# Holding the loads of a second weight matrix behind a store of finer x sums

## The chip, the cores and the metric

The kernel runs on one core of one Trainium2 chip. The metric is the device time in microseconds (us). The engines are named as the profile names them: PE is the matrix engine and PEld its weight loads, DVE the vector engine, ACT the scalar engine, POOL the GpSimd engine and SP the engine that does nothing here but issue DMAs. DMAs issued by SP travel on queue q1 of the profile, those issued by POOL on queue q0.

## The reference

A linear attention is followed by a mixture of eight experts, whose routing table is normalized by eight rounds of alternating row and column sums:

```python
# attention, per batch and head: q, k, v are (8, 8, 576, 64), w_phi is (64, 128)
proj = x @ w_phi
proj = proj - max(abs(proj), axis=-1)
phi = concatenate([exp(proj), exp(-proj)])
kv = k_p.T @ v;  z = k_p.sum(over tokens)
attn = (q_p @ kv) / (q_p @ z + 1e-06)
# experts: x is attn as (N, D) = (4608, 512), E = 8, F = 1024
logits = x @ w_gate
P = exp(logits - logits.max())
for _ in range(8):
    P /= P.sum(1, keepdims=True) + 1e-09
    P /= P.sum(0, keepdims=True) + 1e-09
    P *= N / E
out = 0
for e in range(E):
    h = maximum(x @ w1[e], 0)        # w1[e] is (512, 1024)
    out += P[:, e:e+1] * (h @ w2[e]) # w2[e] is (1024, 512)
```

## The kernel before

The program is first written down as a list of operations, each with the engine that does it, an estimated duration, and the keys that it reads and writes. `Plan.schedule` then simulates all engines and the DMA queues with these estimates, and always takes next the operation that can start first by its own clock, ties going to the one that was written down first. The order that comes out is the order of each engine's instruction stream. On the chip every engine works through its stream in that order; where it needs another engine's result or a landed DMA, it waits on a semaphore, and everything behind it on the same engine waits too. Waits for tiles come from the tile framework; `Op.behind` adds one by hand.

The attention takes about the first 200 us. In it, and for some 45 us after it, PE also works on expert 0 with plain matmuls (L622). From then on experts 1 to 7 are computed with a scheme of seven block products in place of eight, in nine units per expert (two for each pair of token groups (0,1), (2,3), (4,5), (6,7), and one for group 8 alone). This needs sums and differences of blocks of x and of the weights, which DVE makes with `sub` (L1240):

- `sums_x` makes three sums for a pair (into three of the four buffers of the ring X), and stores them to DRAM tiles `xd` (`move_x`, L1422). For three of the blocks of x, named 11, 21 and t1, it calls `fine_x`, which stores the block itself (L1369, L1371) and makes four finer sums of it in one more buffer of ring X, which are stored from there to the DRAM tiles `xi` (L1385; the tile of block t1 appears as `xi0t`, `xi2t`, `xi4t` and `xi6t`, by the pair's first group). With three buffers held by the coarser sums, the finer sums of 11, 21 and t1 take turns in the one that is left: DVE may start on one when the store of the one before has landed.
- Experts 2 to 7 read these sums back from DRAM (`load_fine`, L1397). Expert 1 uses those just made.
- `sums_up` and `sums_down` make the sums of the weights of an expert. `sums_up` of expert 1 follows the finished routing table P; its `sums_down` is written down after the first pair's two units.

`routing` does the eight rounds for P on DVE: row sums (L1164), their reciprocals (L1166), the scaled table (L1167), column sums (L1170), a split into bf16 parts (L1179), a small PE matmul that adds over the partitions (`ps<-cs,colw`, 24 columns), and then L1185, L1188 and L1161. Between them stand DVE's work for expert 0 (L1025) and the x sums of pair (0, 1).

The weights of experts 1 to 7 are loaded by `load_w`, two DMAs of 1 MB (as bf16; from fp32 in DRAM) issued by POOL one straight after the other. `w1` and `w2` have two buffers each; one of each lies in a tile called `wx`, which the attention uses before. So expert 1's weights appear as `wx`, and expert 2's as `w`. POOL's other work in the experts is adding products to the output table (`acc<-acc,hx`, L1875) out of two buffers V that ACT fills (L1872), and smaller sums (L1643).

The main loop begins so:

```python
for e in range(1, E):
    w1, w2 = load_w(e, ["late", ("acc", 4, 0, 0)] if e > 1 else ["late"])
    if e == 1:
        nextX = sums_x(pairs[0])
    A7 = sums_up(e, w1)
    B7 = sums_down(e, w2) if e > 1 else None
```

Of the kernel before, what the change touches and what calls it, by code (L numbers as in the profile page):

```python
# [349 lines left out]
def kernel(  # L350
# [11 lines left out]
    nc = tc.nc  # L362
# [32 lines left out]
    acc = [accp.tile([128, 4, DD], FP32, name=f"acc{g}", tag=f"acc{g}") for g in range(NA)]  # L395
# [12 lines left out]
    late = {}  # L408
# [19 lines left out]
    def dma(queue, nbytes, rate, fn, r=(), w=()):  # L428

        speed, unit = LINK.get(rate, (rate, 40))  # L430
        if nbytes == 2 << 20:
            speed, unit = 400, 150
        o = plan.op(queue, 0.8 if queue == "POOL" else 0.6, 0.0, fn, r, w, (), nbytes / speed)
        o.turn, o.unit = rate == 148, unit

    TI, GR, KM, QM, PM, NM, RM = 0, 0, 0, 0, 0, 0, 0
    R = {}
# [68 lines left out]
    def new(tag):  # L506
        return R[tag].new()
# [3 lines left out]
        return buf().bitcast(BF16)  # L511


    def load_w(e, r=()):
        w1, w2 = new("w1"), new("w2")
        for w, src in ((w1, moe_w1), (w2, moe_w2)):
            dma("POOL", 2 << 20, 280, lambda w=w, src=src: nc.gpsimd.dma_start(
                out=w(), in_=src[e].rearrange("(c p) f -> p c f", p=128)),
                r, [(w, i, j) for i in range(2) for j in range(2)])
        return w1, w2  # L520

    def load_w0(i, r):
# [508 lines left out]
    for b in range(2):  # L1031
# [4 lines left out]
        w=["wphi_f0"])  # L1036
    dma("ACT", 1 << 15, 100, lambda: nc.scalar.dma_start(out=wphi_f[64:128, :], in_=w_phi),
        w=["wphi_f1"])
# [13 lines left out]
    for i in range(2):  # L1052
        dve(450, lambda i=i: nc.vector.memset(vrd[i], 0.0),
            w=[("vrd", i, h, *y) for h in range(2) for y in ((), (1,))])
# [79 lines left out]
    o = plan.op("X", 0.0, 0.0, swap, w=["late"])  # L1134
# [101 lines left out]
    def sub(eng, el, out_, x, y, op, r, w):  # L1236
        f = nc.vector if eng is dve else nc.gpsimd
        kw = {"shared": True} if eng is dve else {}
        eng(el * 0.5 if eng is dve else el * 1.04 + 128,
            lambda: f.tensor_tensor(out=out_(), in0=x(), in1=y(), op=op), r, w, **kw)  # L1240

    def sums_up(e, w1):

        def q(i, j):
            return lambda: w1()[:, 2 * j:2 * j + 2, 512 * i:512 * i + 512]

        S = [None] + [new("T") for _ in range(3)]

        def s(n):
            return lambda: S[n]().rearrange("p (a b) -> p a b", a=2)  # L1250


        a11, a12, a21, a22 = (1, 0), (1, 1), (0, 0), (0, 1)
        late = ["late"] + (["P"] if e == 1 else [])

        def k(a):
            return [(w1, *a)]

        sub(dve, 1024, s(2), q(*a11), q(*a21), ALU.subtract, k(a11) + k(a21) + late, [S[2]])
        sub(dve, 1024, q(*a21), q(*a21), q(*a22), ALU.add, k(a22) + late, k(a21))  # L1260
        sub(dve, 1024, s(1), q(*a21), q(*a11), ALU.subtract, k(a21) + k(a11) + late, [S[1]])
        sub(dve, 1024, s(3), q(*a12), s(1), ALU.subtract, k(a12) + [S[1]] + late, [S[3]])
        A = {"11": (q(*a11), k(a11)), "12": (q(*a12), k(a12)), "22": (q(*a22), k(a22)),
             "s1": (q(*a21), k(a21)), "s2": (s(1), [S[1]]), "s3": (s(2), [S[2]]),
             "s4": (s(3), [S[3]])}
        if e > 1:
            for n in INNER:
                fine_up(A, n)
        return A
# [48 lines left out]
    def xq(gs, i, j):  # L1318

        n = len(gs)  # L1320
        return lambda: xT[:, 2 * i:2 * i + 2, 512 * gs[0]:512 * (gs[0] + n)].rearrange(
            "p k (a b) -> p a k b", a=n)[:, :, :, 256 * j:256 * j + 256]

    def xall(gs):
        return [k for g in gs for k in xkeys(g)]
# [12 lines left out]
    class Turns:  # L1338
# [4 lines left out]
        def next(self):  # L1343
# [16 lines left out]
    Xi = {(g[0], n): dram.tile([128, 7, 256], BF16, name=f"xi{g[0]}{n}")  # L1360
          for g in pairs for n in INNER.values()}
# [3 lines left out]
    def fine_x(gs, n, b, r0):  # L1365

        g = gs[0]
        r = xall(gs) + ["late", *r0]
        dma("SP", 1 << 16, 160, lambda: nc.sync.dma_start(  # L1369
            out=Xi[g, n][:, 0, :], in_=b()[:, 0, 0, :]), r, [("Xi", g, n, 0)])  # L1370
        dma("SP", 1 << 17, 160, lambda: nc.sync.dma_start(  # L1371
            out=Xi[g, n][:, 1:3, :], in_=b()[:, :, 1, :]), r, [("Xi", g, n, 1)])
        y = new("X")

        def t(n):
            return lambda: y().rearrange("p a k c -> p (a k) c")[:, n]

        def blk(k, a):
            return lambda: b()[:, a, k, :]

        sub(dve, 256, t(0), blk(0, 1), blk(0, 0), ALU.subtract, r, [(y, 0), "order of X"])
        sub(dve, 256, t(2), blk(1, 1), blk(0, 1), ALU.subtract, r, [(y, 2)])
        sub(dve, 256, t(1), blk(1, 1), t(0), ALU.subtract, [*r, (y, 0)], [(y, 1)])
        sub(dve, 256, t(3), blk(1, 0), t(1), ALU.subtract, [*r, (y, 1)], [(y, 3)])
        dma("SP", 1 << 18, 160, lambda: nc.sync.dma_start(  # L1385
            out=Xi[g, n][:, 3:7, :], in_=y().rearrange("p a k c -> p (a k) c")),
            [(y, i) for i in range(4)], [("Xi", g, n, 2)])

# [27 lines left out]
    def new_x():  # L1416
        return {n: new("X") for n in (2, 3, 4)}
# [10 lines left out]
    def sums_x(gs, r0=()):  # L1428

        X = new_x()  # L1430

        def x(n):
            return lambda: X[n]()[:, 0:len(gs)]

        b11, b12, b21, b22 = (xq(gs, *ij) for ij in ((0, 1), (0, 0), (1, 1), (1, 0)))
        el, keys = 512 * len(gs), xall(gs)
        r = keys + ["late", *r0]
        sub(dve, el, x(3), b22, b12, ALU.subtract, r, [X[3], "order of X"])
        sub(dve, el, b12, b12, b11, ALU.subtract, ["late", *r0], keys)
        sub(dve, el, x(2), b22, b12, ALU.subtract, r, [X[2]])  # L1440
        sub(dve, el, x(4), b21, x(2), ALU.subtract, r + [X[2]], [X[4], "order of X"])
        for n in (3, 2, 4):
            move_x(gs, n, True, X)
        if len(gs) == 2:
            for n, b in (("22", b22), ("11", b11), ("21", b21), ("t1", b12)):
                if n in INNER.values():
                    fine_x(gs, n, b, r0)
                else:
                    for a in range(2):
                        dma("SP", 1 << 17, 160, lambda n=n, a=a, b=b: nc.sync.dma_start(  # L1450
                            out=Xp[gs[0], n][:, a], in_=b()[:, a]), r, [("Xp", gs[0], n, a)])
        return X
# [524 lines left out]

    early, dn = [plain(8)], plain(7)
    for e in range(1, E):
        w1, w2 = load_w(e, ["late", ("acc", 4, 0, 0)] if e > 1 else ["late"])  # L1980
        if e == 1:
            nextX = sums_x(pairs[0])
        A7 = sums_up(e, w1)
        B7 = sums_down(e, w2) if e > 1 else None
        turn = [*pairs, (8,)] if e < E - 1 else [(8,), *pairs]
        if e == 2:
            o = plan.op("X", 0.0, 0.0, lambda: None, w=["K"])
            for d in plan.ops[:-1]:
                if any(b.ring is R["X"] for b in d.bufs):
                    d.users.append(o)  # L1990
                    o.deps.append(d)
                    o.left += 1
        for n, gs in enumerate(turn):
            if (e, n) == (1, 4):
                plan.inorder = 1
            X = nextX if e == 1 else load_fine(gs)
            H = {g: [] for g in gs}
            for fp in range(len(gs)):
                hs = take()
                for i, z in enumerate(hs):  # L2000
                    H[gs[min(i, len(gs) - 1)]].append(z)
                fine = e > 1 and len(gs) == 2
                if fine:
                    un = up49(A7, fp, X, H, gs, ["up0", "K"])
                else:
                    un = up7(A7, gs, fp, X, H, ["up0"])
                for o in UNITS[turns.pop(0)]:
                    if o in un:
                        un[o]()
                    elif len(o) == 3:  # L2010
                        un[o[:2], int(o[2])]()
                    elif dn is not None:
                        dn[o]()
                if dn is not None:
                    dn["out"]()
                    slots.extend(dn["slots"])
                if e == 1 and fp == 0 and n + 1 < len(turn):
                    nextX = sums_x(turn[n + 1], [(H[gs[0]][0], 0, 1, 1)])
                if B7 is None and fp:
                    B7 = sums_down(e, w2)  # L2020
                if fp == len(gs) - 1:
                    wait += [(e, g, H[g], B7, w2, [z.ring.number for z in H[g]]) for g in gs]
                dn = next_down()
# [35 lines left out]
```

## Time and profile before

| | us |
|---|---|
| median of 3 runs | 1011.01 |
| lowest and highest run | 1009.40 and 1012.25 |
| the profiled execution, its own time | 1010.62 |
| span of the profiled execution | 1008.8 |
| PE busy | 994.0 (99% of the span), 8376 matmuls |
| DVE busy | 898.6 (89%) |
| ACT busy | 812.8 (81%) |
| POOL busy | 447.6 (44%) |
| q1 (issued by SP and ACT) | 103.33 MB, 36.3% of the 16 DMA engines' span |
| q0 (issued by POOL) | 23.86 MB, 16.9% |

All times inside a run are us from the start of the span. A busy share says how long an engine had an instruction in work; PE's matmuls overlap, so its busy time can hide gaps shorter than a matmul's duration, and the starts of the matmuls are the finer measure: a matmul of 512 columns starts 0.216 us after the one before where PE runs without a gap. The granted clock is 1.00 in the whole run. A timeline row gives start, duration, engine, line, operation, tiles, shapes and count, and in brackets the idle time before it and what ended that.

### The profile page before, as it was taken

How to read it: one execution, taken by the hardware profiler on the slowest of the kernel's cores; microseconds unless marked ns; L12 is line 12 of the kernel's file. 1: busy time of each engine (PE TensorE's matmuls, PEld its weight loads, DVE VectorE, ACT ScalarE, POOL GpSimd, SP SyncE). 2: the span in 40 equal slices, each digit the busy share in tenths (PEclk: the TensorE clock that was granted, in tenths of full speed). 3: DMA queues.
4: the chain of work that ended last, by engine and by line, in shares of the span. 5: the costliest groups of instructions: out<-in, count | busy, mean ns of one | idle time of the engine just before them, and what ended most of it. 6: DMA issues, size and time to landing. Idle time of an engine off the chain costs nothing.

```text
span 1008.8 us, 23309 instructions
## 1 busy us (share of the span) xinstructions
PE 994.0 (99%) x8376; PEld 727.7 (72%) x8376; DVE 898.6 (89%) x1999; ACT 812.8 (81%) x1930; POOL 447.6 (44%) x514
## 2 busy tenths in 40 slices
PE   7899999999999999999999999999999999999998
PEld 5666666644566877777777877787778777787775
DVE  7999998987888998899989898989889988989886
ACT  7999999845979788878878788777887888778874
POOL 5778674400133344434444444444443444344443
PEclk9999999999999999999999999999999999999999
DMA  9999999181136423282327133632246222724653
GB/s 249 183 202 183 157 153 144 38 170 56 53 121 143 147 97 98 84 184 96 109 98 170 44 100 131 130 127 98 97 117 177 97 98 84 147 79 142 208 174 126
DMA packets 129748, 128.86 MB, mean 128 GB/s; under 512 B 55776, under 2 KB 98272, under 8 KB 129632
## 3 DMA queue, kind: packets, MB, share of 16 engines
q1 hardware_dynamic: 97680, 103.33, 36.3%
q0 software_dynamic: 31648, 23.86, 16.9%
q8 instruction: 65, 1.06, 0.5%
q14 instruction: 51, 0.42, 0.2%
q10 hardware_dynamic: 304, 0.20, 0.1%
HBM read 122.50 MB, written 19.53 MB: 141 GB/s over the span
## 4 chain that ended last, share of the span: by engine, by line
PE 92%; DVE 3%; ACT 2%; DMA 2%; issue 1%; POOL 0%; DVEq 0%
PE ps L1466 41%; PE ps L1475 20%; PE ps L622 17%; PE ps L1607 11%; PE ps L905 2%; DMA xi6t<-X 1%; DMA xi<-X 1%; PE ps L752 1%; ACT q L618 0%; DVE m L614 0%; ACT k L618 0%; DVE wx L614 0%; DVE X L1240 0%; DMA acc<-in_k_dram 0%; DVE hs L1676 0%
## 5 line engine op out<-in xcount | busy, mean ns | idle before, releaser
L1875 POOL TENSOR_TENSOR acc<-acc,hx 128x512 f32<-128x512 f32 x186 | 236.1, 1276 | 404.7 <-ACT hx L1872 135.0
L1466 PEld LDWEIGHTS <-hs 128*128 128x128 bf16 x1984 | 194.1, 98 | 46.4 <-issue 0.2
L1872 ACT ACTIVATE hx<-ps,P 128x256 f32<-128x256 f32 x372 | 158.9, 483 | 53.4 <-PE ps L1466 52.0
L1860 DVE SCALAR_TENSOR_TENSOR acc<-ps,P,acc 128x256 f32<-128x256 f32 x372 | 162.2, 478 | 30.2 <-PE ps L1466 28.2
L1475 PE MATMUL ps<-xT,T 128*128 128x512 bf16 x608 | 171.0, 379 | 0.0
L1466 PEld LDWEIGHTS <-hx 128*128 128x128 bf16 x1488 | 145.6, 98 | 24.9
L1466 PE MATMUL ps<-hx,hs 128*128 128x256 bf16 x992 | 144.3, 273 | 0.0
L1676 DVE CUSTOM_DVE_ANT_0 hs<-ps,U 128x512 bf16<-128x512 f32 x192 | 124.7, 684 | 11.3 <-PE ps L1475 6.6
L1607 PE MATMUL ps<-xT 128*128 128x256 bf16 x576 | 125.4, 272 | 0.0
L1475 PEld LDWEIGHTS <-T 128*128 128x128 bf16 x672 | 65.8, 98 | 40.6
L1682 ACT ACTIVATE hs<-ps 128x512 bf16<-128x512 f32 x96 | 55.9, 598 | 41.7 <-PE ps L1475 40.2
L1466 PE MATMUL ps<-wx,hs 128*128 128x256 bf16 x560 | 78.4, 273 | 0.0
L622 PE MATMUL ps<-w,hx 128*128 128x512 bf16 x288 | 73.0, 379 | 0.0
L622 PE MATMUL ps<-xT,w 128*128 128x512 bf16 x288 | 72.9, 379 | 0.0
L1466 PE MATMUL ps<-wx,hx 128*128 128x256 bf16 x496 | 72.3, 273 | 0.0
L1676 DVE CUSTOM_DVE_ANT_0 hs<-ps,X 128x512 bf16<-128x512 f32 x96 | 65.1, 684 | 7.8 <-PE ps L1607 6.9
L1466 PE MATMUL ps<-hx 128*128 128x256 bf16 x496 | 71.2, 273 | 0.0
L1607 PEld LDWEIGHTS <-xT 128*128 128x128 bf16 x576 | 56.3, 98 | 17.5
L1466 PE MATMUL ps<-w,hx 128*128 128x256 bf16 x432 | 62.2, 273 | 0.0
L614 DVE TENSOR_REDUCE m<-ps 128x4 f32<-128x512 f32 x88 | 58.8, 680 | 3.7 <-PE ps L622 1.9
L1672 ACT COPY X<-ps 128x512 f32<-128x512 f32 x96 | 58.6, 610 | 2.5 <-DVE ps L1650 2.5
L1466 PE MATMUL ps<-w,hs 128*128 128x256 bf16 x432 | 60.2, 273 | 0.0
(174 smaller groups left out, 2256.0 us busy)
## 6 DMA issues: line engine op xcount, KB each, us to landing
xT<-xi SPq DMA_DIRECT2D x48, 448.0 KB, 4.6
xT<-xd SPq DMA_DIRECT2D x72, 256.0 KB, 4.0
wx<-in_moe_w_dram POOLq DMA_DIRECT2D x8, 1024.0 KB, 11.2
v_m<-in_v_dram SPq DMA_DIRECT2D x15, 512.0 KB, 5.2
out_dram<-acc SPq DMA_DIRECT2D x14, 512.0 KB, 3.0
w<-in_moe_w_dram POOLq DMA_DIRECT2D x6, 1024.0 KB, 11.0
xT<-xp SPq DMA_DIRECT2D x24, 256.0 KB, 2.8
qk<-in_k_dram POOLq DMA_DIRECT2D x12, 256.0 KB, 5.4
```

The source lines that it names most:

```text
L614: dve(el, lambda: nc.vector.tensor_reduce(out=dst(), in_=src(), axis=AX.X, op=ALU.max, apply_absolute_value=True), r, w)
L622: nc.tensor.matmul(out_, lhsT=lhsT, rhs=rhs, start=start, stop=stop)
L905: pe(65, lambda j=j: nc.tensor.matmul(pn()[:, j * D1:j * D1 + D1], lhsT=s["T"][x]()[:, j % 2, 2 * h + j // 2, :] if j < 4 else r["T"][x]() ...
L1466: pe(256, lambda i=i, k=k, z=z: nc.tensor.matmul(bank()[:, 256 * i:256 * i + 256], lhsT=lhs(k, i), rhs=rhs(k), start=first and z, stop=k = ...
L1475: pe(512, lambda k=k: nc.tensor.matmul(bank().rearrange("p (a b) -> p a b", a=2), lhsT=lhs(k), rhs=rhs(k), start=first and k == 0, stop=k ...
L1607: pe(256, lambda: nc.tensor.matmul(halves_of(bank[q], n)(), lhsT=lhs(), rhs=t()[:, rhs, :], start=start, stop=True, skip_group_check=True) ...
L1672: act(512, lambda: nc.scalar.copy(out=flat(to[q])(), in_=bank[q]()), [bank[q]], [(to[q], 0), (to[q], 1)])
L1676: dve(515, lambda: nc.vector._custom_dve(ADD_SAT, out=out_(q, i, j), in0=bank[q]().rearrange("p (a b) -> p a b", a=2), in1=to[q](), s0=3.0 ...
L1682: act(512, lambda: nc.scalar.activation(out=out_(q, i, j), in_=bank[q]().rearrange("p (a b) -> p a b", a=2), func=ACT.Relu, bias=0.0, scal ...
L1860: dve(320, lambda n=n, ts=ts: nc.vector.scalar_tensor_tensor(out=acc[g][:, ts, 256 * j:256 * j + 256], in0=bank()[:, 256 * n:256 * n + 256 ...
L1872: act(370, lambda n=n: nc.scalar.activation(out=u()[:, n, :], in_=bank()[:, 256 * n:256 * n + 256], func=ACT.Copy, bias=0.0, scale=P[:, 4 ...
L1875: pool(695, lambda: nc.gpsimd.tensor_tensor(out=acc[g][:, 2 * i:2 * i + 2, 256 * j:256 * j + 256], in0=acc[g][:, 2 * i:2 * i + 2, 256 * j: ...
```

## The change

`load_w` gets a third argument, the key of a store. The load of `w2` now reads that key for the planner (so it is planned behind the store's landing), and is given `behind`, a real wait on the chip for the landing of that store. The store is that of the four finer sums of block t1: for expert 1 that of pair (0, 1) (`xi0t<-X`), for expert 2 that of pair (6, 7) (`xi6t<-X`). Experts 3 to 7 have none. So that the store is known, `sums_x` of the first pair is now written down ahead of `load_w` for expert 1; and `dma` returns its operation.

```diff
@@ dma
         o.turn, o.unit = rate == 148, unit
+        return o
@@
-    def load_w(e, r=()):
+    written = {}
+
+    def load_w(e, r, store):
         w1, w2 = new("w1"), new("w2")
-        for w, src in ((w1, moe_w1), (w2, moe_w2)):
-            dma("POOL", 2 << 20, 280, lambda w=w, src=src: nc.gpsimd.dma_start(
+        for w, src, behind in ((w1, moe_w1, None), (w2, moe_w2, store)):
+            o = dma("POOL", 2 << 20, 280, lambda w=w, src=src: nc.gpsimd.dma_start(
                 out=w(), in_=src[e].rearrange("(c p) f -> p c f", p=128)),
-                r, [(w, i, j) for i in range(2) for j in range(2)])
+                r + ([behind] if behind else []),
+                [(w, i, j) for i in range(2) for j in range(2)])
+            o.behind = written.get(behind)
         return w1, w2
@@ fine_x
-        dma("SP", 1 << 18, 160, lambda: nc.sync.dma_start(
+        written["Xi", g, n, 2] = dma("SP", 1 << 18, 160, lambda: nc.sync.dma_start(
             out=Xi[g, n][:, 3:7, :], in_=y().rearrange("p a k c -> p (a k) c")),
             [(y, i) for i in range(4)], [("Xi", g, n, 2)])
@@ the main loop
     for e in range(1, E):
-        w1, w2 = load_w(e, ["late", ("acc", 4, 0, 0)] if e > 1 else ["late"])
         if e == 1:
             nextX = sums_x(pairs[0])
+        r = ["late", ("acc", 4, 0, 0)] if e > 1 else ["late"]
+        w1, w2 = load_w(e, r, ("Xi", 6 * (e - 1), "t1", 2) if e < 3 else None)
         A7 = sums_up(e, w1)
```

What this does to the engines' streams, beside the two waits, is small. On POOL the load of expert 2's `w2` stands one L1875 later than before. On DVE the finer sums of blocks 21 and t1 of pair (0, 1) stand earlier among the rounds of the routing: the first of 21 now directly ahead of the column sums (L1170) of the third round, where it stood behind the L1179 of the fourth. On PE the third and the fourth of the eight small matmuls `ps<-cs,colw` each stand two 512-column matmuls later, and two blocks of expert 0 change places. ACT and SP issue the same instructions in the same order. From there to the end every stream is the same, but for four PSUM banks that have changed names.

## The prediction

> **What bounds the kernel now.** I read the page's busy row first, then PE's waits after the attention, because a change that touches nothing before 203 us can only win what PE loses behind it.
>
> ```profile
> PE 994.0 (99%) x8376; PEld 727.7 (72%) x8376; DVE 898.6 (89%) x1999; ACT 812.8 (81%) x1930; POOL 447.6 (44%) x514
> ```
>
> ```profile
> PE ps L1475 <- DVE hs L1530: 0.6, 1, 0.6
> PE ps L622 <- DVE cs L1179: 0.4, 1, 0.4
> ```
>
> PE is busy 99% of the span, and behind 200 us the list of its waits has two entries. Busy time hides short gaps, so I also took the starts of all matmuls and subtracted the pace without gaps (0.216 us for 512 columns, 0.1085 for 256). At the first wait PE loses 0.52 us at 227.4 and 0.13 at 228.6; at the second 0.79 at 329.2 and 0.17 at 330.4. That is 1.6 us in all, and the rest of the 800 us behind them has hardly a gap. **No version of this change can win more than about 1.6 us, 0.16%.**
>
> Next, the timeline around both places, DVE, PE and the loads:
>
> ```profile
> 203.41 1.74 POOL L517 DMA_DIRECT2D wx<-in_moe_w_dram  x2 [7.21 <-PE ps L622]
> 217.08 0.32 SPq L1385 DMA_DIRECT2D xi<-X  x1
> 223.50 0.49 DVE L1240 TENSOR_TENSOR X<-xT 128x256 bf16<-128x256 bf16 x2 [1.49 <-DMA xi<-X]
> 228.10 0.19 PE L622 MATMUL ps<-cs,colw 128*128 128x24 bf16 x1 [0.36 <-DVE cs L1179]
> 316.00 1.69 POOL L517 DMA_DIRECT2D w<-in_moe_w_dram  x2
> 317.00 0.32 SPq L1385 DMA_DIRECT2D xi6t<-X  x1
> 324.77 0.42 DVE L1240 TENSOR_TENSOR X<-xT 128x512 bf16<-128x512 bf16 x1 [1.01 <-DMA xi6t<-X]
> 330.20 1.19 PE L1475 MATMUL ps<-X,wx 128*128 128x512 bf16 x4 [0.62 <-DVE hs L1530]
> ```
>
> Both waits of PE have one pattern. POOL issues two weight loads; a store of finer sums issued during them takes long to land (217.08 to 223.48, 6.40 us; 317.00 to 324.75, 7.75 us, where such stores take 2.0 us at other times); DVE stands idle for the buffer (1.49 and 1.01 us); and what DVE makes then comes late for PE.
>
> The third view is a window of 2 us (busy time of the five engine rows, granted clock, share of the DMA engines, GB/s), and the fourth the landings of the POOL loads of the tiles `wx` and `w`.
>
> ```profile
> 220.00:222.00 2.00, 2.00 (x11) 0.94 (x10) 1.83 (x6) 0.87 (x2) 0.00 (x0) 1.00 1.10 364
> ```
>
> ```profile
> DMA to landing us min/median/max: 10.4/13.8/17.2
> DMA to landing us min/median/max: 9.5/11.9/14.3
> ```
>
> By single DMAs, expert 1's are issued at 203.41 and 204.25 and land at 213.77 and 221.47; expert 2's at 316.00 and 316.79 and land at 325.55 and 331.10. So the two go one after the other: q0's bytes reach 1.05 MB at 212.6 and 2.10 MB at 220.3. While they last the stores get 0.07 to 0.1 MB/us; when the second is through, 0.31 to 0.37 (the 364 GB/s of the row 220 to 222).
>
> **Expert 1's hold.** What it removes: `w2` no longer moves from 212.6 to 220.3. What it doesn't: `w1` is in front, so up to 212.6 all is as before, and q1 has then moved 0.32 MB. Adding the stores in SP's order, the 256 KB store `xi<-X` of block 11 (217.08 before) ends at 1.77 MB. 1.77 less 0.32 at 0.34 MB/us takes 4.3 us: its bytes are through at 216.9. SP can issue it in time: it waits for the store eight places ahead (0.52 MB, through at 213.2, landed about 1.2 us later by the landings before), so at about 214.4. Landings follow the last byte by 0.8 to 1.2 us: it lands between 217.6 and 218.0, in place of 223.48.
>
> But the order now asks for it sooner. DVE's first finer sum of block 21 stands ahead of the third round's L1170, which before started at 216.69. So DVE waits there from 216.67 to about 217.8, in the middle of the rounds, where before it waited after the fourth round. From that landing to the third small matmul it is 0.2 us for the sub, 1.21 for L1170 to the second L1179 with two subs between (the same sequence took 207.92 to 209.13), and 0.09 of latencies: 1.50, so 219.3. PE, which ran it at 218.03, now stands two matmuls of 0.216 later: 218.46. PE loses 0.84 us. The fourth comes 20 matmuls (4.34 us) later for PE, at 223.6, and DVE has it ready at about 223.3 (c_bc to the next L1179 took 218.62 to 222.02, 3.4 us). The fifth: PE at 228.4, DVE at about 228. So the 0.65 lost at 227 to 229 goes, and 0.84 comes 9 us earlier: **+0.2 us**. The bounds: a landing before 216.96 costs nothing and gives -0.65; one 0.5 us later than 218.0 gives +0.9.
>
> The load itself: the t1 store lands about 226.6 (DVE is through with it some 4 us earlier than the 228.80 of its issue before, and it takes 2.0 us), POOL issues then in 0.87 us, and by the 9.5 to 10.4 us of a first load it lands about 237. DVE reads it first at 259.15, PE at 266.35: 22 us of cover, which is what would have to go before this costs anything. On POOL nothing else is queued until the L1875 at 269.95.
>
> **Expert 2's hold.** Here the first load, too, is in front of the store. By 324.5 q0 had moved 0.99 MB, all of it `w1`; so the store's 7.75 us were spent beside `w1` alone, and holding `w2` doesn't shorten them. DVE's 1.01 us and PE's 0.96 stay: **0**. The other bound is -0.96, if the mere queueing of `w2` held the store back.
>
> New is that POOL stands at the wait from 320.95 (the end of the L1875 that starts at 319.68) to 324.75, then issues for 0.87 us; the second L1875 of that pair, before at 320.95, starts at 325.63. Who waits for that: ACT's next fill of a V buffer, at 332.80, so 5.9 us of cover behind its end at 326.9. But it now falls into a run of DVE subs from 324.77 to 329.5 without a gap, which ends in the L1530 that PE waits for at 330.20. What POOL and DVE do to each other the trace shows nearby:
>
> ```profile
> 342.25 1.27 POOL L1875 TENSOR_TENSOR acc<-acc,hx 128x512 f32<-128x512 f32 x1 [1.17 <-ACT ps L1527]
> 342.62 1.18 DVE L1240 TENSOR_TENSOR hs<-hs 128x512 bf16<-128x512 bf16 x1
> 338.43 1.24 DVE L1240 TENSOR_TENSOR xT<-w,xT 128x256 bf16<-128x256 bf16 x1
> ```
>
> The sub at 342.62 takes 1.18 us, its kind 0.42 otherwise, and ends 0.28 after the POOL add; that at 338.43 takes 1.24 for 0.29. Between 275 and 343 I find six such subs, at 0.33 to 0.95 us too long, mean 0.63. DVE is the chain here, so PE pays it: **+0.6**, between 0 (the add slips into a gap) and 1.27 (a whole add). [...]
>
> `w2` of expert 2 lands at about 335 to 337 rather than 331.10; DVE reads it at 365.2. It now runs beside the loads `xT<-xi` issued from 329.99 and takes some us from them; these landed at 333.57 to 341.57, and PE's first uses are at 348.9, 349.1 and 351.2, 14 to 15 us behind the landings of their blocks. Nothing.
>
> **The sum.** +0.2 +0.6 = +0.8 on the profiled execution: 1010.62 to 1011.4. That execution lies 0.4 below the median, 1011.01, so for the median 1011.8. Both are inside 0.3% (3.0 us), about what a measurement of this kernel can tell from no change.
>
> **Rivals.** (1) The waits vanish. If the store lands before DVE asks, expert 1 gives -0.65; if expert 2's store is also quicker without the queued `w2` and the POOL add does no harm, another -0.96: 1010.4 to 1009.4. For it: the stores run at four times the pace as soon as `w2` is out of the way. Against it: the 216.9 above, and `w1` still being there both times. 30%. (2) Slower: the wait moved into the rounds is long. DVE now stops at 216.67 for a landing whose time before was 223.48, and from 216.96 on each us of its delay is one of PE's. Were the stores not sped up at all, PE would stand 6.5 us, less 0.65: 1016.9. It passes 0.3% if the landing is later than 220.6. For it: at 215 to 219 eight stores are queued, and SP's own waits for landings space them. Against it: at 220.3, with the loads through, 0.7 MB went in 2 us. 8%. (3) The hold is idle, both waits of PE stay as they are: 1011.0, 7%. My forecast has 55%.
>
> **How the numbers follow.** The low end is rival 1 in full, -1.6: 1009.4. The high end takes both upper bounds, +0.9 and +1.27, and a little of the 1.2 us by which the runs lie above the median: 1013.4. The chance of slower by over 0.3% is rival 2's, 8%; faster by over 0.3% exceeds what PE loses at these places and could only be scatter, 3%; the rest, 89%, is within.
>
> **What would show it.** Right: DVE's wait for `xi<-X` stands ahead of a column sum at 217 to 218, of 1 us, and PE waits 0.6 to 1.1 for the third `ps<-cs,colw`, none at 228; `xi6t<-X` takes over 7 us again; an L1875 starts at about 325.6 and a sub near it is 0.3 to 1 us too long. Wrong: `xi<-X` landing before 217 or after 220.6; `xi6t<-X` landing by 321; a wait of PE at a place that has none now, above all for `w` or `hx` behind 332, where POOL's delayed add would be the cause.

## The result and the profile after

| | before | after |
|---|---|---|
| median (18 runs each, us) | 1010.12 | 1012.41 |
| lowest and highest run | 1009.25, 1012.25 | 1011.23, 1015.05 |
| ratio of the times | | 1.0025, 95% interval 1.0017 to 1.0032 |
| profiled execution, its own time and span | 1010.62, 1008.8 | 1011.88, 1010.1 |

The change costs a quarter of a per cent: it is slower, and by the medians the loss lies inside the 0.3% that the forecast called "within". The line numbers of after are 5 higher (the POOL add L1875 is now L1880, a `sub` L1245, PE's second wait L1480 on L1535). The busy row of the page, in which 36 of PE's matmuls have no record, and PE's waits behind 200 us:

```profile
PE 991.9 (98%) x8340; PEld 727.8 (72%) x8376; DVE 900.1 (89%) x1999; ACT 813.4 (81%) x1930; POOL 448.2 (44%) x514
```

```profile
PE ps L1480 <- DVE hs L1535: 2.1, 1, 2.1
PE ps L627 <- DVE cs L1184: 0.3, 1, 0.3
PE ps L1471 <- DVE hx L1245: 0.3, 1, 0.3
```

The two waits of before, 0.6 and 0.4, have become one of 2.1 and two of 0.3 (of these the one on `cs` stands at expert 1's place, the one on `hx` at expert 2's). By the starts of the matmuls, with the pace taken off as in the prediction, PE loses 0.45 us at expert 1's place (0.65 before) and 0.43 + 2.29 + 0.17 = 2.89 at expert 2's (0.96 before). That is -0.20 and +1.93. The rest of the stream runs as before, except that this execution comes 0.41 us earlier out of the attention, which the change does not touch: -0.20 + 1.93 - 0.41 = 1.32, and the spans differ by 1.3.

Expert 1's place in the timeline (start, duration, engine, line, operation, tiles, and in brackets the idle time before it and what ended it):

```profile
217.00 0.29 DVE L1245 TENSOR_TENSOR X<-xT 128x256 bf16<-128x256 bf16 x1 [0.76 <-DMA xi<-X]
217.21 0.67 DVE L1175 TENSOR_REDUCE cs<-T 128x8 f32<-128x288 f32 x1
...
226.02 0.89 POOL L520 DMA_DIRECT2D wx<-in_moe_w_dram  x1 [22.18 <-DMA xi0t<-X]
```

The store that DVE waits for was issued at 213.79 and landed at 216.98, 6.5 us sooner than before. DVE now waits ahead of the column sum L1175 of the third round, 0.76 us, as the new order asks for. The held load goes out at 226.02, lands at 236.06, and nobody waits for it.

Expert 2's place, POOL, DVE and PE:

```profile
324.68 0.93 POOL L520 DMA_DIRECT2D w<-in_moe_w_dram  x1 [4.35 <-ACT U L1528]
325.62 1.28 POOL L1880 TENSOR_TENSOR acc<-acc,hx 128x512 f32<-128x512 f32 x1
```

```profile
324.16 0.42 DVE L1245 TENSOR_TENSOR X<-xT 128x512 bf16<-128x512 bf16 x1 [1.02 <-DMA xi6t<-X]
324.51 0.42 DVE L1245 TENSOR_TENSOR hx<-hs,hx 128x512 bf16<-128x512 bf16 x1
324.84 2.35 DVE L1245 TENSOR_TENSOR xT<-xT 128x512 bf16<-128x512 bf16 x1
327.12 0.41 DVE L1245 TENSOR_TENSOR hs<-hs 128x512 bf16<-128x512 bf16 x1
...
331.53 0.59 PE L1480 MATMUL ps<-X,wx 128*128 128x512 bf16 x2 [2.13 <-DVE hs L1535]
```

The store of `xi6t` landed at 324.14, 7.76 us after its issue (7.75 before). DVE waits 1.02 us for it, as before. Then the held load is issued (its bracket names ACT, which had long been done; it waits for the landing at 324.14, and its row begins 0.54 behind that), the add follows directly at 325.62, and one subtraction takes 2.35 us in place of 0.42. It ends 0.29 after the add does, and it began 0.78 before the add's row. PE gets its operand later by both sums: 1.02 + 1.93 = 2.95, against 2.89 lost.

### The profile page after: what moved, and what is told of

Same layout as the page of the kernel before. It is cut to its first block, busy times and chain, and to the rows that moved or that the text cites. A ratio compares the mean times of both kernels' runs of the same rounds, so it can differ in the third digit from the quotient of the medians.

```text
span 1010.1 us, 23276 instructions
## 1 busy us (share of the span) xinstructions
PE 991.9 (98%) x8340; PEld 727.8 (72%) x8376; DVE 900.1 (89%) x1999; ACT 813.4 (81%) x1930; POOL 448.2 (44%) x514
## 4 chain that ended last, share of the span: by engine, by line
PE 92%; DVE 3%; ACT 3%; DMA 1%; issue 1%; DVEq 0%
PE ps L1471 41%; PE ps L1480 20%; PE ps L627 17%; PE ps L1612 11%; PE ps L910 2%; ACT q L623 1%; DMA xi6t<-X 1%; ACT k L623 1%; PE ps L757 0%; DVE m L619 0%; DVE wx L619 0%; DMA xi<-X 0%; DMA acc<-in_k_dram 0%; DVE X L1245 0%; DVE hs L1681 0%
## 5 line engine op out<-in xcount | busy, mean ns | idle before, releaser
L1880 POOL TENSOR_TENSOR acc<-acc,hx 128x512 f32<-128x512 f32 x186 | 236.3, 1277 | 379.1 <-ACT hx L1877 115.9
L1480 PE MATMUL ps<-xT,T 128*128 128x512 bf16 x608 | 171.1, 379 | 0.0
L1480 PEld LDWEIGHTS <-T 128*128 128x128 bf16 x672 | 65.7, 98 | 40.7 <-issue 0.2
L627 PE MATMUL ps<-xT,w 128*128 128x512 bf16 x271 | 70.2, 379 | 0.6
L627 PE MATMUL ps<-w,hx 128*128 128x512 bf16 x275 | 69.9, 379 | 0.5
```

The lines of the kernel that those rows point to most:

```text
L627: nc.tensor.matmul(out_, lhsT=lhsT, rhs=rhs, start=start, stop=stop)
L1480: pe(512, lambda k=k: nc.tensor.matmul(bank().rearrange("p (a b) -> p a b", a=2), lhsT=lhs(k), rhs=rhs(k), start=first and k == 0, stop=k ...
L1880: pool(695, lambda: nc.gpsimd.tensor_tensor(out=acc[g][:, 2 * i:2 * i + 2, 256 * j:256 * j + 256], in0=acc[g][:, 2 * i:2 * i + 2, 256 * j: ...
```

## The experiments

The question was what the 1.93 us are made of, whether each hold does what was expected of it, and why the runs of after differ among themselves by more than those of before. In the kernels that reorder POOL's work, `done` is the list that the planner returns, `w1` and `w2` are the two load operations of expert 2, `add` is the L1880 that stands behind the held load in after, and `also` is a second wait beside `behind`. The edits are shortened. Nothing else differs: unless said otherwise, the streams of the other engines are those of after.

### One hold at a time

```diff
# e1_only
-("Xi", 6 * (e - 1), "t1", 2) if e < 3 else None
+("Xi", 6 * (e - 1), "t1", 2) if e < 2 else None
# e2_only
+("Xi", 6 * (e - 1), "t1", 2) if e == 2 else None
```

> The hold of expert 1 alone; expert 2's loads as before. Theory A (the loss comes from expert 2's hold, by what POOL then does beside DVE): PE loses about 0.45 us at the third small matmul in place of the 0.65 of before, and 0.79 and 0.17 at 329 as before, so 0.2 us faster than before, 1009.9 against 1010.1. Rival B (the late second matrix or the new order of the routing costs something behind it, in all the runs): 1 to 2 us slower than before, 1011 to 1012.

> The hold of expert 2 alone; expert 1 as before. Theory A: PE loses 0.65 us at 227 to 229 as before and 2.9 us at 327 to 331 (0.43, 2.29, 0.17) in place of 0.96, so 1.9 us slower than before, 1012.0; a DVE sub at about 325 takes 2.35 us. Rival B: near before, 1010.1 to 1010.5, and no long sub.

Measured: expert 1's hold alone 1010.92 us, ratio to before 1.0005 (0.9996 to 1.0014); expert 2's alone 1012.16, ratio 1.0025 (1.0015 to 1.0035), as much as the whole change. The first has a store of `xi6t` that takes 7.8 us and PE's loss of 0.85 + 0.17 at 328 to 330; the second loses 0.53 + 2.29 + 0.17 there, with the same subtraction of 2.35 us. So the cost is expert 2's. The 0.2 us by which expert 1's hold alone was expected to be faster don't show: its median lies 0.7 above that of before, and the interval includes no change.

The second run showed something that no theory had. The rows give, for a window of 4 us, the busy time of PE, PEld, DVE, ACT and POOL (with the count of instructions), the granted clock, the DMA share and GB/s; after first, which has the same gap of PE just ahead of the window, then expert 2's hold alone:

```profile
331.50:335.50 4.00, 3.96 (x30) 2.93 (x30) 4.00 (x14) 2.57 (x6) 0.00 (x0) 1.00 1.12 309
```

```profile
331.50:335.50 4.00, 4.00 (x18) 2.38 (x17) 3.22 (x11) 1.48 (x3) 0.00 (x0) 0.61 1.11 322
```

With expert 2's hold alone, where PE's gap of 2.29 us ends at 331.36, the granted clock falls to 0.61 in the mean of this window (by the trace's clock it is 0.50 from 332.41 to 335.82, for 3.41 us), and 18 matmuls run where 30 do in after. In that stretch each matmul of 256 columns starts about 0.1 us later behind the one before than the usual 0.1085: some 1.6 us in all. The profiled execution of after keeps a clock of 1.00.

### What holds the subtraction: the load's issue, the add, or both

```diff
# add_first: on POOL the add goes ahead of the held load
+done.remove(w2); done.insert(done.index(add) + 1, w2)
# add_held: w2 goes out at once behind w1; the add waits for the store instead
+done.remove(w2); done.insert(done.index(w1) + 1, w2)
+add.also, w2.behind = w2.behind, None
```

> As the changed kernel, every other stream alike, but on POOL the held load of expert 2's second matrix and the add behind it change places, so that the add runs at once and only the issue of the load stands at the wait. Theory A1 (issue and add hold DVE up one after the other): the sub at 324.8 waits for the end of the issue alone and takes 1.0 to 1.1 us in place of 2.35; PE loses about 1.4 at 329; the time lies 1.3 us below the changed kernel and 0.4 to 0.5 above before. Theory A2 (only the add holds DVE up): the sub takes 0.42, PE loses 0.79 at 329, the time is 1.9 below the changed kernel and 0.2 below before.

> As the changed kernel, but the load of expert 2's second matrix is issued unheld behind that of the first, as before, and the wait for the store stands on the add that followed it. No issue is near DVE's run at 324; the add alone is. Theory A1: the add starts within 0.1 us of the landing, beside the first subs; one sub is 0.3 to 1.3 us too long, PE loses 1.1 to 2.1 at 329; 0.1 to 1.1 slower than before. Theory A3 (only the issue holds DVE up): no long sub, PE loses 0.79, 0.2 faster than before. In all of them the store lands 7.7 us after its issue, as it did in both kernels.

The first, 1010.79 us, ratio 1.0009 (1.0000 to 1.0018):

```profile
324.75 0.93 POOL L530 DMA_DIRECT2D w<-in_moe_w_dram  x1 [2.98 <-PE ps L1491]
```

```profile
324.58 0.42 DVE L1256 TENSOR_TENSOR hx<-hs,hx 128x512 bf16<-128x512 bf16 x1
324.92 0.42 DVE L1256 TENSOR_TENSOR xT<-xT 128x512 bf16<-128x512 bf16 x1
325.25 0.42 DVE L1256 TENSOR_TENSOR hs<-hs 128x512 bf16<-128x512 bf16 x1
```

The same issue in the same burst of subtractions, and all of them take their 0.42 us. The issue alone holds nothing. PE's loss at 329 is that of before, 0.95; the median is 0.6 above that of before, though, where 0.2 below was expected. The second, 1011.83 us, ratio 1.0016 (1.0007 to 1.0026):

```profile
324.40 1.42 POOL L1892 TENSOR_TENSOR acc<-acc,hx 128x512 f32<-128x512 f32 x1 [4.57 <-ACT U L1540]
```

```profile
324.61 1.49 DVE L1257 TENSOR_TENSOR hx<-hs,hx 128x512 bf16<-128x512 bf16 x1
326.02 0.41 DVE L1257 TENSOR_TENSOR xT<-xT 128x512 bf16<-128x512 bf16 x1
```

The add alone holds a subtraction up by 1.07 us, most of its own length. Neither gives the 1.93 of after. What is left is the add standing ready behind the issue while the issue runs. Two more kernels moved the moment at which the add becomes ready. Each was executed once, under the profiler (1011.58 and 1012.96 us), so their traces count here and not their times:

```diff
# add_third, add_second: subs are DVE's subtractions behind the landing of xi6t
+done.remove(add); add.also = subs[2]      # add_second: subs[1]
+done.insert(done.index(subs[2]) + 1, add)
```

> As after, but the POOL add behind expert 2's w2 load waits for the third subtraction after the store of xi6t has landed (X, hx, xT), so that no add is ready behind the issue while it runs. Theory P (a ready add that stands behind the issue already holds the subtractions off): the third subtraction takes its 0.42 us; once it ends, near 325.25, the add is ready while the issue still runs to 325.6, so the fourth subtraction is held from 325.2 to 327.2, 1.6 us too long. Theory Q (the hold begins at the add's own start): the fourth subtraction takes 0.42 us and the fifth, begun near 325.5, is held for about 1.3 us. By both the burst of subtractions ends about 1.6 us later than without the add (after: 1.93), PE's loss at 329 is 2.3 to 2.6 us instead of after's 2.89, and the span 1009.5 to 1010.0, 1.7 more if the granted clock falls behind the gap.

> As add_third, but the POOL add behind expert 2's w2 load waits for the second subtraction after the landing of xi6t (X, hx) instead of the third. In add_third the add became ready only when the fourth subtraction had begun, so it could not tell the theories apart; here it is ready about 0.3 us sooner, near 325.3 on add_third's times, while the issue still runs to 326.0 and before the fourth subtraction begins at 325.5. Theory P (a ready add behind the running issue already holds the subtractions off): the third takes its 0.42 us, the fourth is held until 0.3 us behind the add's end, 1.5 us too long. Theory Q (only the add itself holds them, from about its own start): the fourth takes 0.42 us and the fifth is held, 1.2 to 1.3 us too long, as in add_third. By both PE's loss at 329 stays near 2.1 to 2.4 us.

In the first of them the fourth subtraction (324.53, 324.87, 325.21, 325.54) took 0.42 us and the fifth 1.68, begun at 325.88 ahead of an add at 325.99. But the third ended at 325.63, so the add was not ready before the fourth had begun, and this run decides nothing. The second tells them apart:

```profile
324.51 0.93 POOL L532 DMA_DIRECT2D w<-in_moe_w_dram  x1 [4.47 <-PE ps L1493]
325.46 1.28 POOL L1893 TENSOR_TENSOR acc<-acc,hx 128x512 f32<-128x512 f32 x1
```

```profile
324.68 0.42 DVE L1258 TENSOR_TENSOR xT<-xT 128x512 bf16<-128x512 bf16 x1
325.01 2.02 DVE L1258 TENSOR_TENSOR hs<-hs 128x512 bf16<-128x512 bf16 x1
326.96 0.41 DVE L1258 TENSOR_TENSOR hx<-hx,hs 128x512 bf16<-128x512 bf16 x1
```

The subtraction that the add waits for, the second, ends at 324.76; the third, begun at 324.68, runs through in 0.42; the fourth, begun at 325.01 with the add now ready and the issue running to 325.44, stands until 327.03, 1.60 us too long and 0.45 of it before the add's row. That is what theory P says and Q does not: **in these traces an add that stands ready behind a running DMA issue on POOL already keeps DVE's subtractions out, and the price is the rest of the issue plus nearly the whole add** (0.45 + 1.28 less 0.13 here, 0.78 + 1.28 less 0.13 in after and in expert 2 alone). It rests on one execution of each of these three kernels. How the chip does it, or whether the profile dates the add's row late, the runs don't show.

Why this add had no wait of its own can be read from the planner. It keeps POOL's adds and DVE's subtractions apart: it plans them one after the other, and an add that is planned to start within 1.5 us behind a subtraction gets a real wait on it through `behind`. In the plan of after the store of `xi6t` has landed by 316.9, and the add runs from 318.5 to 319.8 with no wait, ahead of the burst of subtractions, which is planned from 320.5 on (the planner's clock is some 2.6 us ahead of the trace here: DVE's work in front of the burst ends at 323.14 in the trace). On the chip the store landed at 324.14 and let the burst and the held load go together. An add that waits for the end of the burst was not tried.

With that, PE's loss at this place follows from two terms of DVE in each kernel:

| | DVE's wait for xi6t | the held subtraction | sum | PE's loss |
|---|---|---|---|---|
| add_first | 1.00 | 0 | 1.00 | 0.95 |
| expert 1 alone | 1.08 | 0 | 1.08 | 1.02 |
| add_third | 0.94 | 1.26 | 2.20 | 2.14 |
| add_held | 1.32 | 1.07 | 2.39 | 2.34 |
| add_second | 1.14 | 1.60 | 2.74 | 2.67 |
| after | 1.02 | 1.93 | 2.95 | 2.89 |
| expert 2 alone | 1.13 | 1.93 | 3.06 | 2.99 |

And behind the longest gaps the clock falls in some executions: in the profiled ones of expert 2 alone, add_held and add_second (gaps of 2.29, 2.17 and 2.29 us; each time a clock of 0.50 for 3.41 us, and about 1.6 us lost by the slowed matmuls), not in those of after and add_third (2.29 and 1.97). In the four kernels with such a gap of over 2.1 us, 14 of 36 executions had a mean granted clock of 0.998; of 120 executions of before and of the kernels without such a gap, 5 had 0.998 or less, so such a mean is much more frequent with the gap, and the gap is not the only way there. Where the clock fell is seen in the profiled executions alone. In after the ten executions at 1.000 have a median of 1012.33 and the six at 0.998 one of 1013.94. So at a clock of 1.000 the change costs about 2.2 us, of which the trace accounts for 1.73. The rest, 0.5, stays open: expert 1 alone and add_first have medians 0.7 and 0.6 above before, too, though their traces lose 0.2 to 0.3 us less than before at these places. The fall of the clock would account for what is added in a third of the runs of after.

### What the hold would be worth without the load in front

```diff
# w1_early: expert 2's w1 goes out behind expert 1's w2, once PE has read its buffer
# for the last time; w2 stays held, behind the add
+done.remove(w1); done.insert(last_reader + 1, w1)
+done.remove(w2); done.insert(done.index(add) + 1, w2)
# w1_early_free: the same w1; w2 goes out where w1 did, without a wait (here
# last_reader and w1_old_place stand for places in the list)
+done.insert(w1_old_place, w2); w2.behind = None
# w1_early_none: the same as w1_early_free, and expert 1's w2 isn't held either;
# the other engines' streams are those of before
```

> Both holds stay, but expert 2's w1 is issued right behind expert 1's w2 near 227 instead of at 315.4, and the POOL add goes ahead of expert 2's held w2. Theory A (the store of xi6t is slow because w1's load runs in front of it): the store lands 2.0 us after its issue at 316.4, near 318.4, DVE does not wait for it, PE's gaps of 0.96 us at 327 to 332 are gone; w2 is issued near 321.7 and lands by 332. The stores at 245 to 246 run beside w1's last microsecond. Against before -0.2 (expert 1) and -0.96: near 1009.0, ratio 0.9988. Theory B (the stall at 329 comes from elsewhere, or another wait takes its place at once): the store lands in 2.0 us but PE still loses about 1 us between 320 and 335, 1010.0.

> As w1_early, but expert 2's w2 is not held: it is issued at about 315.4, where w1's load was, and the hold of expert 1 stays. Theory A: the store of xi6t runs beside w2's load and lands about 7.8 us after its issue, at 324.1, and PE loses its 0.96 us at 327 to 332 as before: 1009.9, ratio 0.9998; the difference to w1_early, about 0.9 us, is what the hold is worth where nothing else runs in front of the store. Theory B: no difference to w1_early.

> Neither load is held; all streams are those of before, but for expert 2's loads on POOL: w1 is issued behind expert 1's w2, once PE has read its buffer for the last time (near 236), and w2 alone at 315 to 316. By the runs so far the stall of 0.96 us at 327 to 332 is gone, as in w1_early_free, and PE's 0.65 at 227 to 229 is that of before: 1009.0 to 1009.4, ratio 0.9990; against w1_early_free, whose expert 1 hold was worth 0.2 to 0.3 us in the trace, no difference that the runs can show. The other theory, that the hold of expert 1 is part of what made w1_early_free quicker than before by 0.8: 1010.2, ratio 1.0.

| | time, us | ratio to before | `xi6t` lands after | PE's loss at 227 and at 329 |
|---|---|---|---|---|
| w1_early | 1009.43 | 0.9992 (0.9983 to 1.0001) | 2.00 | 0.47, 0 |
| w1_early_free | 1009.36 | 0.9992 (0.9983 to 1.0001) | 6.32 | 0.29, 0 |
| w1_early_none | 1009.39 | 0.9994 (0.9985 to 1.0003) | 6.23 | 0.58, 0 |

(PE's first loss stands at 218 where expert 1's load is held.) The tile `xi6t`, first with `w1` early and `w2` held, then with `w2` free:

```profile
DMA to landing us min/median/max: 2.0/2.0/2.0
```

```profile
DMA to landing us min/median/max: 6.3/6.3/6.3
```

Without `w1` in front the store takes 2.0 us, as the theory said, and DVE's first subtraction follows without a wait. In the second kernel the theory missed. The store does run beside a load, `w2` this time, but lands in 6.3 us rather than 7.8, at 323.08, and DVE comes to it at 323.44. So it is hidden by 0.36 us, and holding `w2` is worth nothing even here. The third kernel answers the last question: expert 1's hold, 0.2 to 0.3 us in the trace, doesn't show in the time. All three are about 3 us below after: their slowest run took 1010.69, the fastest of after 1011.23. Against before the three intervals each end just above 1, so the 0.4 to 0.8 us by which their medians are lower are not proved.

## Why the time fell within the range, and which terms were wrong

**What bounds the kernel, and the pattern of both waits:** right. PE's loss at the two places was what the change moved in the trace, and the seven kernels of the table bear out that it is DVE's delay, passed on whole.

**Expert 1, +0.2:** the mechanism was right, the term mis-sized. The wait did move ahead of the third round's column sum, and the loss at 227 to 229 went. The store landed at 216.98 where 217.6 to 218.0 was worked out; 0.4 of that is the earlier start of this execution. PE loses 0.45 instead of 0.84, so in the trace the term is -0.20: within its bounds, but a gain where a loss was forecast. The time of expert 1's hold alone doesn't show it.

**Expert 2's stall, 0:** right. The store took 7.76 us, since `w1` is in front of it; with `w1` gone it took 2.00.

**The add pushed into DVE's burst, +0.6:** this is the step that failed. It was mis-sized by a factor of three, and its upper bound, "a whole add", was too low as well: 1.93 against 1.27. The six rows it was taken from were adds with no DMA issue in front; here the add stands behind one, and add_held, where it doesn't, measured 1.07, inside the bounds. The start of the add's row is not the moment from which it keeps the other out: the held subtraction of after began 0.78 us before it. That the add started at 325.62, as forecast (325.6), is a coincidence: the store landed 0.61 earlier than before, and the add started 1.48 behind the landing where 0.88 had been worked out.

**What was left out:** the clock. The prediction treated PE's gap as its own length. Behind gaps of 2.17 to 2.29 us there were 3.41 us at a clock of 0.50 in three of four profiled executions. What makes it fall, and why only some executions show it, no run shows.

**The sum and the rivals:** +0.8 was forecast; the trace has -0.20 + 1.93 = +1.73, the medians +2.29, nearly three times as much. The forecast of 1011.8 stands only 0.6 below the 1012.41 because its base (1011.01 from three runs) turned out 0.9 above the median of 18: that it came so near was luck. The waits did not vanish (rival 1), since `w1` was still there and the add did do harm; the wait in the rounds was short (rival 2), because the landing came only 0.76 us after DVE asked for it; and both holds act (rival 3). Of its signs of being right two were missed: the long subtraction is 1.93 us too long where 0.3 to 1 was given, and PE's loss at the third small matmul is 0.45 where 0.6 to 1.1 was given. Of its signs of being wrong one came by the letter: `xi<-X` landed at 216.98, before 217, though on the clock of before, 0.41 later, that is 217.39. The others, `xi6t` landing by 321 and a wait behind 332 for POOL's later add, did not come.

## What to carry to other kernels

When a transfer is held back on a queue, look at what stands behind it on the issuing engine and when that becomes ready: released in one go, the issue and the add behind it fell together into the one burst that PE was waiting for, and that cost 1.93 us beside a stall of 0.96. The plan had kept the add and the burst apart by its own times alone, and the late landing undid that. Holding the second load did not help a store that the first already slowed (7.76 us from issue to landing with the hold, 7.75 without, 2.00 with the first out of the way); issuing the first 80 us sooner removed the stall without any wait. And a new gap on PE may cost more than its length: here, behind gaps of 2.17 to 2.29 us, about 1.6 us more in three of four profiled executions.

## What was not expected of the hardware

- A subtraction on DVE was held from before the row of a POOL add that stood ready behind a DMA issue: 0.78 us before it in after and in expert 2 alone, 0.45 in add_second; an issue of 0.93 us with no add ready behind it held nothing, and an add alone held 1.07.
- Behind PE gaps of 2.17 to 2.29 us the granted clock fell to 0.50 for 3.41 us in three of four profiled executions, which cost about 1.6 us each time.
- The store of `xi6t` takes 2.00 us by itself, 7.7 to 8.1 beside the load of `w1` and 6.2 to 6.3 beside that of `w2`, though both loads have the same bytes. Why was not tried.
- A load on POOL that waits for a store has its row begin 0.53 to 0.54 us behind the landing (in after 226.02 behind 225.48, and 324.68 behind 324.14); DVE's subtraction starts 0.02 behind the same landing.
